# One cyclic table for the order of work on every engine, gated values split a stream at a time, and a convolution that runs further ahead

## The chip, the cores and the metric

The kernel runs on one NeuronCore of a Trainium2 chip. The core has five engines, each with a queue of its own that it works through strictly in order: TensorE (PE, matrix products into PSUM), VectorE (DVE), ScalarE (ACT), GpSimd (POOL) and SyncE (SP), which here issues nearly all the DMA transfers. Engines wait for one another through semaphores. The metric is the time of one execution on the device in microseconds (us). Three runs of the kernel before gave 443.19, 444.54 and 445.52, median 444.54. One more execution was profiled: it took 444.06, with a span of 442.2 from its first instruction to its last.

## The reference

An input `x` of 8 x 4224 tokens x 192 features goes through two convolutions over time, a gate and two products:

```python
w = softmax(weight)                      # 8 heads x 7 taps, one head per 24 features
out[b,s,h,:] = sum_k w[h,k] * x_pad[b,s+k,h,:]
x = out                                  # the first result is the input of the second part
gate_pre = sum_k conv_w[k] * xp[:, k:k+S, :]      # 5 taps, a weight per feature
gate = 1 / (1 + exp(-gate_pre))
val = x @ w_val                          # 192 x 192
result = (gate * val) @ w_out            # 192 x 192
```

## The kernel before, in words

**Tiling.** The 8 sequences are laid end to end, four to a row of blocks, so each block covers up to 488 tokens of two rows. There are 35 blocks (`STEPS`, numbered 0 to 34; the last has 380 tokens) in ten groups: group 0 has blocks 0 and 1, groups 1 to 8 four blocks each, group 9 the last. The 192 features times two rows make three *streams* of 128 partitions: streams 0 and 1 are the first 128 features of the two rows (together `x1`, one 976-wide tile), stream 2 holds the other 64 features of both rows (`x2`).

**First convolution.** It is made on PE, in units (`conv_unit`, L257): eight matmul records into one PSUM bank `pc` (L270), a copy by ACT into a buffer `e` (L276, six buffers), and one or two transfers that scatter `e` into `x1` or `x2` of the group (L280). Two of every three units belong to `x1`, the third to `x2`. A group of four blocks has 12 units, all units together are 106. After each third unit two more input tiles are loaded (`load_x`, L137; eight buffers, seven loaded at the start). `x1` and `x2` have three buffers, one for a group.

**Second convolution.** Each stream of each block has an accumulator in PSUM (`pg`, two banks for all). ACT makes the first tap into it (`tap0`, L315), DVE adds taps 1 to 4 (`tap`, L327), of which the last writes to `g` in SBUF; ACT then applies the sigmoid in place (L335; streams 0 and 1 in one instruction). So there are 12 taps on DVE for a block. Two taps of one stream are mostly set apart by a tap of the next (`taps`, L339).

**Products.** `val` and the output are products with a weight cut in four parts: `W11` and `W22` within the two feature ranges, `W12` and `W21` across. An f32 operand is split in two fp32r parts, a high one that ACT casts (`xh`, `ph`, L356) and a rest that POOL subtracts (`xl`, `pl`, L357), and each product is three matmuls. The 64-wide `W12` is used in plain f32 (`columns`, L393). The other parts are `rows` (`W21`, L402), `whole1` (`W11`, L411) and `whole2` (`W22`, L419). Every product of a block adds up in three banks, one for a stream: `pv` for the value, `po` for the output. `pv`, `po` and the convolution's `pc` share six banks, taken in turn: whoever opens a bank waits until the one opened six before has been read. DVE multiplies `pv` with the gate in place (`gated`, L432), ACT evacuates `po` into `ot` (L438), and SP stores a block's three streams with one transfer (L442).

**Order.** The order on every engine is written out by hand. `pair(n)` (L444) makes the value products of blocks n and n+1 and the output products of blocks n-1 and n, with six convolution units between its two halves. In its first half each product part of the value is followed by the same part of the output: `columns`, `rows`, `whole2`, `whole1`; in the second half the order is `whole1`, `whole2`, `rows`, `columns`. The gating of streams 0 and 1 of block n+1 follows `v2.rows` there. A prologue does 6, 3 and 3 units, then block 0's and block 1's first steps around six more, 18 units in all, so that units 12 to 17 come after block 0's taps and value product. Then come the pairs n = 1, 3, ..., 33 and an epilogue that makes the last block's output product. Group 1 (blocks 2 to 5, units 6 to 17) is first read early in pair 1, group 2 early in pair 5, and so on every second pair.

Of the kernel before, what the change touches and what calls it, by code (L numbers as in the profile page):

```python
# [7 lines left out]
F32 = mybir.dt.float32  # L8
F32R = mybir.dt.float32r
# [25 lines left out]
MB = 488  # L35
# [39 lines left out]
GROUP = [max(1, 4 // nj) for nj in NJS]  # L75
XW = 768
# [4 lines left out]
def kernel(  # L81
# [170 lines left out]
    def bank(name):  # L252
        return ps_v.tile([128, 512], F32, tag="pv", name=name)
# [3 lines left out]
    def conv_unit(g, u):  # L257
# [5 lines left out]
        pc = bank(f"pc_{g}_{u}")  # L263
        m, run = p.rows[i], p.wins[i] * WIN
        for k, h in enumerate(hs):
            t, o = xtiles[g, h]
            o += p.off[i]
            for w in range(p.wins[i]):
                c = k * run + w * WIN
                nc.tensor.matmul(  # L270
                    pc[:m, c : c + WIN], lhsT=t[:, o + w * m : o + w * m + m], rhs=band[:, h, :],
                    start=True, stop=True,
                )
        e = ep.tile([128, MB], F32, tag="e", name=f"e_{g}_{u}")
        n = run * len(hs)
        nc.scalar.copy(e[:m, :n], pc[:m, :n])  # L276
# [4 lines left out]

    units = [(g, u) for g in range(NG) for u in range(len(PLANS[g].units))]
    done = [0]

    def conv(k=1):
        for _ in range(k):
            if done[0] < len(units):
                g, u = units[done[0]]
                conv_unit(g, u)
                done[0] += 1  # L290
                i, hs = PLANS[g].units[u]
                if i == 1 and (hs[-1] + 1) % GROUP[g] == 0:
                    load_x(len(hs) // GROUP[g])
# [17 lines left out]
    def tap0(n, i):  # L311
        if n < N:
            m = STEPS[n][2]
            acc = accs[n, i] = ps_g.tile([128, 512], F32, tag="pg", name=f"pg_{n}_{i}")[:, :m]
            nc.scalar.mul(acc, unit_view(n, i, 0), cwt[:, i // 2, 0:1])  # L315

    def tap(n, i, k):
        if n >= N:
            return
# [12 lines left out]
    def sigmoid(n, i):  # L332
        if n < N:
            v = (g1s, g2s)[i][n]
            nc.scalar.activation(v, v, AF.Sigmoid)  # L335

    order = [(n, i) for n in range(1, N + 2) for i in (2, 0, 1)]

    def taps(n, i):  # L339


        k = order.index((n, i))
        nxt, opened = order[k + 1], order[k + 2]
        tap(n, i, 3)
        tap(*nxt, 1)
        tap(n, i, 4)
        tap(*nxt, 2)
        tap0(*opened)

    def split(pool, tag, n, i, x):  # L350
        m = STEPS[n][2]
        if i == 0:
            h, l = (pool.tile([128, 2, MB], F32R, tag=t, name=f"{tag}{t}_{n}")[:, :, :m] for t in ("h", "l"))
        else:
            h, l = (pool.tile([128, MB], F32R, tag=t, name=f"{tag}{t}_{n}")[:, :m] for t in ("h2", "l2"))
        nc.scalar.copy(h, x)  # L356
        nc.gpsimd.tensor_tensor(out=l, in0=x, in1=h.bitcast(F32), op=ALU.subtract)  # L357
        return h, l

    def split_x(n, i):  # L360
        if n < N:
            xs[n, i] = split(sp, "x", n, i, views(n)[i])

    def split_g(n, i):
        ps[n, i] = split(pp, "p", n, i, (g1s, g2s)[i][n])
# [3 lines left out]
    class Product:  # L369
# [18 lines left out]
        def columns(self):  # L388
# [9 lines left out]
        def rows(self):  # L398
# [8 lines left out]
        def whole1(self):  # L407
            first, both = self.open(0, 1)
            for q, acc in enumerate(both):
                for i, (a, b) in enumerate(self.passes(0)):  # L410
                    nc.tensor.matmul(  # L411
                        acc, lhsT=a[:, W11 : W11 + 128], rhs=b[:, q],
                        start=first and i == 0, stop=not first and i == 2,
                    )

        def whole2(self):
# [7 lines left out]
    def value(n):  # L424
        return Product(w_val, n, "pv", views(n)[0], xs, pvs)

    def output(n):
        return Product(w_out, n, "po", g1s[n], ps, pos)
# [5 lines left out]
    def evacuate(n, q):  # L434
        m = STEPS[n][2]
        if n not in ots:
            ots[n] = op.tile([128, 3 * MB], F32, tag="ot", name=f"ot_{n}")
        nc.scalar.copy(ots[n][:, q * m : (q + 1) * m], pos.pop((n, q)))  # L438

    def store(n, a=0, b=3):  # L440
        m = STEPS[n][2]
        nc.sync.dma_start(out[:, AT[n] + a * m : AT[n] + b * m], ots[n][:, a * m : b * m])  # L442

    def pair(n):  # L444
        m = n + 1
        v, o, v2, o2 = value(n), output(n - 1), value(m), None

        v.columns()
        split_g(n - 1, 1)
        taps(n, 0)  # L450
        o.columns()
        split_g(n - 1, 0)
        split_x(m, 0)
        v.rows()
        o.rows()
        taps(n, 1)
        sigmoid(n, 0)

        v.whole2()
        gated(n, 2)  # L460
        o.whole2()
        evacuate(n - 1, 2)
        split_x(m, 1)
        taps(m, 2)
        sigmoid(m, 1)
        v.whole1()
        split_g(n, 1)
        gated(n, 0)
        gated(n, 1)
        o.whole1()  # L470
        evacuate(n - 1, 0)
        evacuate(n - 1, 1)
        store(n - 1)
        split_g(n, 0)
        conv()
        taps(m, 0)
        conv(2)
        taps(m, 1)
        sigmoid(m, 0)
        conv(2)  # L480
        split_x(n + 2, 1)
        conv()
        split_x(n + 2, 0)
        taps(n + 2, 2)
        v2.whole1()
        o2 = output(n)
        o2.whole1()
        v2.whole2()
        o2.whole2()
        sigmoid(n + 2, 1)  # L490

        v2.rows()
        gated(m, 0)
        gated(m, 1)
        o2.rows()
        evacuate(n, 0)
        evacuate(n, 1)
        v2.columns()
        gated(m, 2)
        o2.columns()  # L500
        evacuate(n, 2)
        store(n)

    with tc.manual_schedule(engines={ENG.SP, ENG.PE, ENG.Activation, ENG.DVE, ENG.Pool}):
# [5 lines left out]
        conv(3)  # L510
        w_out.split()
        order[:0] = [(0, i) for i in (2, 0, 1)]
        tap0(0, 2)
        tap0(0, 0)
        split_x(0, 1)
        split_x(0, 0)
        tap(0, 2, 1)
        tap(0, 2, 2)
        taps(0, 2)
        conv(3)  # L520
        taps(0, 0)
        sigmoid(0, 1)
        v = value(0)
        v.columns()
        v.whole2()
        v.rows()
        v.whole1()
        for i in (1, 0):
            split_x(1, i)
        taps(0, 1)  # L530
        sigmoid(0, 0)
        conv(6)
        for q in (2, 0, 1):
            gated(0, q)
        taps(1, 2)
        sigmoid(1, 1)
        for n in range(1, N, 2):
            pair(n)
        split_g(LAST, 1)
        split_g(LAST, 0)  # L540
        o = output(LAST)
        o.columns()
        o.rows()
        o.whole2()
        evacuate(LAST, 2)
        store(LAST, 2, 3)
        o.whole1()
        for q in range(2):
            evacuate(LAST, q)
            store(LAST, q, q + 1)  # L550
# [68 lines left out]
```

## Time and profile before

| | |
|---|---|
| runs, median | 444.54 us (443.19 to 445.52) |
| profiled execution | 444.06 us, of it 442.2 span |
| mean granted TensorE clock | 0.956 |
| POOL, busiest line L357 | 122.3 us on `pl`, 112.0 us on `xl` |
| DVE, busiest line L327 | 218.6 us into `pg`, 75.0 us into `g` |
| HBM read, written | 28.33 MB, 26.01 MB |

The table of engines on the profile's page gives busy time, its share of the span and the number of instructions. PE is the matmuls, PEld the loading of their weights, which overlaps them. Names such as `po<-ph,woh` are what an instruction writes and reads. A bracket behind an instruction gives the idle time of its engine just before it, and what ended that. In the list of waits the three numbers are the total, how many times, and the longest.

### The profile page before, as it was taken

Reading aid. Unit: us, or ns where it says so; the run is one execution under the profiler, and the core shown is the slowest. Engines: PE = TensorE matmul, PEld = TensorE weight load, DVE = VectorE, ACT = ScalarE, POOL = GpSimd, SP = SyncE. Lnnn points to the kernel's source line nnn. Section 1 sums busy time; section 2 is a strip of 40 time slices with the busy share of each in tenths; the row PEclk is TensorE's granted clock in tenths of the full one; section 3 lists DMA queues with packets and bytes.
Section 4 is the critical chain, followed back from the end, with each engine's and each line's share of the span. In section 5 each row is a group of like instructions: output and inputs, shape, how many; then the busy total and the mean of one; then the engine's idle time right before and its main releaser. Section 6 shows DMA issues by size and latency. Waiting matters only on the chain.

```text
span 442.2 us, 7292 instructions
## 1 busy us (share of the span) xinstructions
PE 378.2 (86%) x2458; PEld 296.2 (67%) x2458; DVE 346.9 (78%) x572; ACT 322.2 (73%) x533; POOL 238.4 (54%) x155
## 2 busy tenths in 40 slices
PE   1758738999898989998898989898988898996965
PEld 1645527786777677867685959585957695864753
DVE  5159619797979597969797979797979797989851
ACT  2237419787888598859787988698869788887743
POOL 0215107564756384738473847384738473856652
PEclk9896967999999989999999999999999999998987
DMA  6899963939494939393949493939493936232113
GB/s 135 215 231 238 237 148 126 286 131 285 136 280 145 268 106 290 136 260 119 267 164 268 152 292 134 277 128 274 148 244 151 266 125 183 82 104 88 70 68 120
DMA packets 38805, 81.55 MB, mean 184 GB/s; under 512 B 7280, under 2 KB 25072, under 8 KB 38768
## 3 DMA queue, kind: packets, MB, share of 16 engines
q1 hardware_dynamic: 38512, 80.59, 64.3%
q0 software_dynamic: 256, 0.50, 0.5%
q8 instruction: 19, 0.31, 0.3%
q14 instruction: 18, 0.15, 0.1%
HBM read 28.33 MB, written 26.01 MB: 123 GB/s over the span
## 4 chain that ended last, share of the span: by engine, by line
PE 32%; DVE 20%; DMA 15%; issue 14%; ACT 11%; POOL 4%; SPq 2%; POOLq 0%; ACTq 0%; DVEq 0%
DMA x<-e 12%; DVE pg L327 11%; PE pc L270 6%; PE po L411 6%; DVE g L327 5%; DMA x<-xw 3%; PE pv L402 3%; PE pv L393 3%; ACT g L335 3%; POOL pl L357 3%; PE po L419 3%; PE pv L419 3%; DVE g L432 3%; ACT e L276 3%; PE po L402 3%
## 5 line engine op out<-in xcount | busy, mean ns | idle before, releaser
L327 DVE SCALAR_TENSOR_TENSOR pg<-x,cwt,pg 128x486 f32<-128x486 f32 (+2 forms) x315 | 218.6, 722 | 24.5 <-ACT pg L315 22.3
L357 POOL TENSOR_TENSOR pl<-g,ph 128x486 fp32r<-128x486 f32 (+2 forms) x70 | 122.3, 1747 | 106.8 <-ACT ph L356 100.1
L357 POOL TENSOR_TENSOR xl<-x,xh 128x486 fp32r<-128x486 f32 (+2 forms) x70 | 112.0, 1614 | 72.1 <-ACT xh L356 71.1
L270 PE MATMUL pc<-band,x 128*128 128x122 f32 (+1 forms) x848 | 104.3, 284 | 15.5 <-DMA band<-row 9.3
L270 PEld LDWEIGHTS pc<-band,x 128*128 128x128 f32 (+1 forms) x848 | 103.1, 200 | 18.1 <-issue 13.4
L315 ACT ACTIVATE pg<-x,cwt 128x488 f32<-128x488 f32 (+2 forms) x105 | 70.7, 673 | 60.3 <-DVE g L327 30.5
L432 DVE TENSOR_TENSOR g<-pv,g 128x488 f32<-128x488 f32 (+2 forms) x105 | 66.1, 658 | 44.6 <-PE pv L402 38.1
L438 ACT COPY ot<-po 128x488 f32<-128x488 f32 (+2 forms) x105 | 55.1, 558 | 30.0 <-PE po L402 14.0
L327 DVE SCALAR_TENSOR_TENSOR g<-x,cwt,pg 128x488 f32<-128x488 f32 (+2 forms) x105 | 75.0, 715 | 0.0
L276 ACT COPY e<-pc 128x488 f32<-128x488 f32 x106 | 56.8, 569 | 23.6 <-PE pc L270 14.6
L335 ACT ACTIVATE g<-g 128x486 f32<-128x486 f32 (+2 forms) x70 | 55.8, 798 | 1.7 <-DVE g L327 1.7
L356 ACT CAST xh<-x 128x486 fp32r<-128x486 f32 (+2 forms) x70 | 55.8, 803 | 0.0
L356 ACT CAST ph<-g 128x486 fp32r<-128x486 f32 (+2 forms) x70 | 55.4, 792 | 0.0
L411 PE MATMUL po<-ph,woh 128*128 128x486 f32 (+2 forms) x70 | 29.7, 424 | 26.4 <-ACT e L276 14.9
L393 PE MATMUL pv<-x,wvf 128*64 128x244 f32 (+2 forms) x280 | 36.4, 381 | 4.0 <-DMA x<-xw 4.0
L411 PE MATMUL po<-pl,woh 128*128 128x486 f32 (+2 forms) x70 | 29.8, 426 | 10.2 <-POOL pl L357 10.2
L411 PEld LDWEIGHTS po<-ph,woh 128*128 128x128 f32 x70 | 13.7, 196 | 34.9 <-ACT e L276 19.8
L393 PE MATMUL po<-g,wof 128*64 128x244 f32 (+2 forms) x280 | 34.4, 367 | 0.0
L393 PEld LDWEIGHTS pv<-x,wvf 128*64 128x64 f32 x280 | 18.7, 138 | 16.6 <-issue 10.0
L411 PE MATMUL pv<-xh,wvh 128*128 128x486 f32 (+2 forms) x70 | 29.0, 414 | 0.0
L411 PE MATMUL po<-ph,wol 128*128 128x486 f32 (+2 forms) x70 | 28.0, 399 | 0.0
L411 PE MATMUL pv<-xl,wvh 128*128 128x486 f32 (+2 forms) x70 | 27.5, 394 | 0.0
(67 smaller groups left out, 395.5 us busy)
## 6 DMA issues: line engine op xcount, KB each, us to landing
x<-xw SPq DMA_DIRECT2D x70, 384.0 KB, 6.1
x<-e SPq DMA_DIRECT2D x64, 244.0 KB, 5.3
out<-ot SPq DMA_DIRECT2D x18, 729.0 KB, 5.4
out<-ot SPq DMA_DIRECT2D x16, 732.0 KB, 3.2
x<-e SPq DMA_DIRECT2D x72, 122.0 KB, 5.8
out<-ot SPq DMA_DIRECT2D x3, 190.0 KB, 1.9
band<-row SPq DMA_DIRECT2D x8, 61.0 KB, 5.2
x<-e POOLq DMA_DIRECT2D x8, 61.0 KB, 7.6
```

Source lines behind the costliest of these rows:

```text
L270: nc.tensor.matmul(pc[:m, c : c + WIN], lhsT=t[:, o + w * m : o + w * m + m], rhs=band[:, h, :], start=True, stop=True,)
L276: nc.scalar.copy(e[:m, :n], pc[:m, :n])
L315: nc.scalar.mul(acc, unit_view(n, i, 0), cwt[:, i // 2, 0:1])
L327: nc.vector.scalar_tensor_tensor(out=dst, in0=unit_view(n, i, k), scalar=cwt[:, i // 2, k : k + 1], in1=acc, op0=ALU.mult, op1=ALU.add,)
L335: nc.scalar.activation(v, v, AF.Sigmoid)
L356: nc.scalar.copy(h, x)
L357: nc.gpsimd.tensor_tensor(out=l, in0=x, in1=h.bitcast(F32), op=ALU.subtract)
L393: nc.tensor.matmul(acc[p, c], lhsT=self.w.f[:, W12 : W12 + 64], rhs=self.x1[:, q, c], start=first and i == 0, stop=not first and i == 1,)
L402: nc.tensor.matmul(acc, lhsT=a[p, W21 : W21 + 128], rhs=b[p], start=first and i == 0, stop=not first and i == 2,)
L411: nc.tensor.matmul(acc, lhsT=a[:, W11 : W11 + 128], rhs=b[:, q], start=first and i == 0, stop=not first and i == 2,)
L432: nc.vector.tensor_tensor(out=v, in0=pvs.pop((n, q)), in1=v, op=ALU.mult)
L438: nc.scalar.copy(ots[n][:, q * m : (q + 1) * m], pos.pop((n, q)))
```

## The change

Four things change; what is computed stays the same.

1. *The table.* The hand-written `pair`, `taps` and most of the prologue and epilogue go. A text `SCHEDULE` lists the steps of a window, which again covers two blocks, n and n+1, and `window(n)` works through it for n = -5, -3, -1, 1, ..., 35, leaving out steps of blocks that don't exist. A step has a kind, an argument and an offset to n: `V` and `O` are value and output products with the part (`110` and `111` are `whole1` of stream 0 and of stream 1, now apart), `T` a tap (stream, tap), `Z` the first tap, `S` the sigmoid, `G` the gating, `E` the evacuation (a block's third one also stores), `CX` and `XL` cast and rest of `x` (1 or 2 for `x1` or `x2`), `CG` and `GL` cast and rest of the gated values, `U` the matmuls of a convolution unit, `K` its copy and scatter.
2. *Gated values a stream at a time.* `CG` and `GL` work on one stream, so that the 976-wide instructions of streams 0 and 1 become two of 488 each. The split of `x1` stays in one.
3. *Units in two parts.* `conv_unit` becomes `conv_begin` and `conv_end`, and in a window the copy of a unit comes one or two units after its matmuls.
4. *Further ahead.* 12 units come before window(-3) and six before window(-1); three more follow window(1) and three window(3). `U` and `K` do nothing in the windows up to -1. The table also casts `x1` one block earlier: `CX1+2` and `CX1+3` where the pair had n+1 and n+2.

By engine the table reads:

```
PE    V12+0 O12-1 V21+0 O21-1 V22+0 V110+0 V111+0 O22-1 O110-1 O111-1 U0 U1 U2 U3 U4 U5
      V110+1 V111+1 V22+1 O22+0 O110+0 O111+0 V21+1 O21+0 V12+1 O12+0
DVE   T11+0 T04+0 T12+0 T13+0 T21+1 T14+0 T22+1 G2+0 T23+1 G0+0 T24+1 T11+1 G1+0 T12+1 T01+1
      T13+1 T02+1 T14+1 T03+1 T04+1 T21+2 T22+2 T23+2 T01+2 T02+2 T24+2 T03+2 G0+1 G1+1 G2+1
ACT   CG2-1 E2-2 Z2+1 S2+0 CX2+1 CG1-1 S0+0 Z1+1 CX1+2 E2-1 CG0+0 Z0+1 K0 E0-1 K1 E1-1 K2 K3
      CG2+0 Z2+2 K4 CG1+0 K5 Z0+2 CX1+3 S2+1 S0+1 CX2+2 Z1+2 E0+0 CG0+1 E1+0
POOL  GL2-1 GL0-1 GL1-1 XL2+1 XL1+1 GL0+0 GL2+0 GL1+0 XL1+2 XL2+2
```

The core of the diff, with the lines that only rename left out:

```diff
+SCHEDULE = """
+    V12+0 T11+0 CG2-1 T04+0 E2-2 O12-1 GL2-1 T12+0 Z2+1 V21+0 T13+0 S2+0 GL0-1 O21-1 CX2+1 T21+1
+    CG1-1 T14+0 V22+0 GL1-1 T22+1 V110+0 S0+0 G2+0 V111+0 XL2+1 Z1+1 T23+1 O22-1 CX1+2 G0+0 O110-1
+    XL1+1 T24+1 E2-1 O111-1 T11+1 CG0+0 U0 Z0+1 G1+0 U1 T12+1 K0 GL0+0 E0-1 T01+1 U2 K1 T13+1 E1-1
+    U3 T02+1 K2 U4 T14+1 K3 T03+1 CG2+0 U5 Z2+2 GL2+0 T04+1 V110+1 K4 T21+2 CG1+0 V111+1 K5 T22+2
+    GL1+0 V22+1 Z0+2 T23+2 O22+0 CX1+3 XL1+2 T01+2 O110+0 S2+1 T02+2 O111+0 S0+1 T24+2 V21+1 CX2+2
+    T03+2 O21+0 Z1+2 XL2+2 G0+1 V12+1 G1+1 E0+0 CG0+1 O12+0 E1+0 G2+1
+"""
...
+    def part_g(n, q):
+        if q < 2:
+            return [t[:, q] for t in halves(ps, pp, "p", n, 0)] + [g1s[n][:, q]]
+        return halves(ps, pp, "p", n, 1) + [g2s[n]]
+
+    def cast_g(n, q):
+        h, _, x = part_g(n, q)
+        cast(h, x)
...
+    def window(n):
+
+        for step, arg, at in SCHEDULE:
+            if step == "U":
+                if n > 0:
+                    conv_begin()
+            elif step == "K":
+                if n > 0:
+                    conv_end()
+            elif 0 <= n + at < N:
...
-        conv(3)
+        conv(6)
         w_out.split()
...
+        window(-5)
+        window(-3)
         conv(6)
...
+        window(-1)
+        for n in range(1, N + 2, 2):
+            window(n)
+            if n < 4:
+                conv(3)
```

More of the change, by code (lines that the diff above doesn't have):

```diff
@@ L1 @@
+import re
 from contextlib import ExitStack
@@ L255, with conv_begin @@
     ISSUERS = {(0, 1): nc.gpsimd}
-    def conv_unit(g, u):
+    units = [(g, u) for g in range(NG) for u in range(len(PLANS[g].units))]
+    begun, ended, opened = [0], [0], {}
+    def conv_begin():
+        if begun[0] == len(units):
+            return
+        g, u = units[begun[0]]
+        begun[0] += 1
         p = PLANS[g]
@@ L273, in conv_unit, with conv_end @@
                 )
+    def conv_end():
+        if ended[0] == begun[0]:
+            return
+        g, u = units[ended[0]]
+        ended[0] += 1
+        p = PLANS[g]
+        i, hs = p.units[u]
+        m, run = p.rows[i], p.wins[i] * WIN
         e = ep.tile([128, MB], F32, tag="e", name=f"e_{g}_{u}")
         n = run * len(hs)
-        nc.scalar.copy(e[:m, :n], pc[:m, :n])
+        nc.scalar.copy(e[:m, :n], opened.pop((g, u))[:m, :n])
         dst = (x1s[g], x2s[g])[i].rearrange("p (s t) -> p s t", t=run)
@@ L405, in rows, with part11, part22 @@
                     )
[L407 to L416, printed above, removed]
+        def part11(self, q):
+            first, (acc,) = self.open(q)
+            for i, (a, b) in enumerate(self.passes(0)):
+                nc.tensor.matmul(
+                    acc, lhsT=a[:, W11 : W11 + 128], rhs=b[:, q],
+                    start=first and i == 0, stop=not first and i == 2,
+                )
+        def part22(self):
             first, (acc,) = self.open(2)
@@ L422, in whole2, with part, product @@
                 )
[L424 to L428, printed above, removed]
+        def part(self, k):
+            (self.part12, self.part21, self.part22)[("12", "21", "22").index(k)]() if len(k) == 2 else self.part11(
+                int(k[2])
+            )
+    products = {}
+    def product(kind, n, k):
+        if (kind, n) not in products:
+            products[kind, n] = (
+                Product(w_val, n, "pv", views(n)[0], xs, pvs) if kind == "V"
+                else Product(w_out, n, "po", g1s[n], ps, pos)
+            )
+        products[kind, n].part(k)
     def gated(n, q):
@@ L436, in evacuate @@
         if n not in ots:
[L437 to L502, printed above, removed]
@@ new lines, in evacuate @@
+            ots[n] = op.tile([128, 3 * MB], F32, tag="ot", name=f"ot_{n}"), []
+        ot, full = ots[n]
+        nc.scalar.copy(ot[:, q * m : (q + 1) * m], pos.pop((n, q)))
+        full.append(q)
+        a, b = (q, q + 1) if n == LAST else (0, 3) if len(full) == 3 else (0, 0)
+        if b:
+            nc.sync.dma_start(out[:, AT[n] + a * m : AT[n] + b * m], ot[:, a * m : b * m])
+    STEP = {"V": product, "O": product, "G": gated, "E": evacuate, "Z": tap0, "T": tap, "S": sigmoid,
+            "CX": cast_x, "XL": rest_x, "CG": cast_g, "GL": rest_g}
```

117 lines of the change are left out of this document (37 added, 80 removed).

## Prediction, with its working

> **What bounds the kernel now.** I read the page first, then the busy time by stage (the windows view), then who waited for whom, then one pair of blocks in order of time, and last the two ends of the span.
>
> ```profile
> span 442.2 us, 7292 instructions
> PE 378.2 (86%) x2458; PEld 296.2 (67%) x2458; DVE 346.9 (78%) x572; ACT 322.2 (73%) x533; POOL 238.4 (54%) x155
> ```
>
> No engine fills the span, so the stages have to be looked at one by one. I cut the span where `v.columns` of pair 3 and of pair 33 begin. Columns: length, then busy time of PE, PEld, DVE, ACT, POOL, then the granted clock, DMA share and GB/s.
>
> ```profile
> 0.00:83.73 83.73, 52.98 (x307) 43.48 (x309) 46.51 (x99) 39.86 (x67) 25.42 (x27) 0.86 0.84 195
> 83.73:413.59 329.86, 304.68 (x2038) 238.15 (x2036) 286.74 (x452) 268.36 (x442) 200.44 (x120) 0.99 0.64 189
> 413.59:442.20 28.61, 20.55 (x117) 14.57 (x113) 13.68 (x25) 14.02 (x24) 12.53 (x8) 0.86 0.25 99
> ```
>
> The middle row is pairs 3 to 31, fifteen of them: 329.86 / 15 = 21.99 us a pair. PE is busy 304.68 / 15 = 20.3 of it, DVE 19.1, ACT 17.9. So three engines stand close together and PE is nearest to full. What keeps them from being full is seen in the waits:
>
> ```profile
> DVE g L432 <- PE pv L402: 38.1, 17, 5.4
> DVE pg L327 <- ACT pg L315: 22.3, 7, 10.7
> ACT pg L315 <- DMA x<-e: 16.3, 3, 11.8
> PE po L411 <- ACT e L276: 14.9, 12, 1.3
> ```
>
> Once a pair, DVE waits for `v2.rows` before it can gate (38.1 / 17 = 2.2 us), and in most pairs PE waits over a microsecond for a bank that ACT's convolution copy gives back. One pair in order of time:
>
> ```profile
> 300.47 0.49 PE L411 MATMUL po<-ph,woh 128*128 128x486 f32 x1 [1.12 <-ACT e L276]
> ...
> 305.98 0.99 PE L393 MATMUL pv<-x,wvf 128*64 128x242 f32 x8
> ...
> 310.68 0.38 PE L411 MATMUL pv<-xh,wvh 128*128 128x486 f32 x1
> ...
> 313.35 5.51 PE L270 MATMUL pc<-band,x 128*128 128x122 f32 x48
> ...
> 318.63 0.47 PE L411 MATMUL pv<-xh,wvh 128*128 128x488 f32 x1
> ...
> 322.18 0.49 PE L411 MATMUL po<-ph,woh 128*128 128x486 f32 x1 [1.30 <-ACT e L276]
> ```
>
> The same matmul returns after 322.18 - 300.47 = 21.71, and it waited 1.30, so without that wait PE needs 20.41 for a pair. Its parts: one half's products 313.35 - 305.98 = 7.37, the six convolution units 318.63 - 313.35 = 5.28, or 0.88 a unit. DVE over the same pair:
>
> ```profile
> 300.90 0.72 DVE L327 SCALAR_TENSOR_TENSOR pg<-x,cwt,pg 128x486 f32<-128x486 f32 x1
> 303.77 1.24 DVE L432 TENSOR_TENSOR g<-pv,g 128x488 f32<-128x488 f32 x2 [2.15 <-PE pv L402]
> 305.37 0.67 DVE L432 TENSOR_TENSOR g<-pv,g 128x488 f32<-128x488 f32 x1 [0.36 <-PE pv L393]
> ...
> 315.38 1.36 DVE L327 SCALAR_TENSOR_TENSOR pg<-x,cwt,pg 128x488 f32<-128x488 f32 x2
> 316.64 0.72 DVE L327 SCALAR_TENSOR_TENSOR g<-x,cwt,pg 128x488 f32<-128x488 f32 x1
> 317.28 2.13 DVE L327 SCALAR_TENSOR_TENSOR pg<-x,cwt,pg 128x488 f32<-128x488 f32 x3
> 319.31 0.72 DVE L327 SCALAR_TENSOR_TENSOR g<-x,cwt,pg 128x488 f32<-128x488 f32 x1
> ...
> 322.60 0.72 DVE L327 SCALAR_TENSOR_TENSOR pg<-x,cwt,pg 128x486 f32<-128x486 f32 x1
> ```
>
> From 300.90 to 322.60 it is 21.70, of which 2.15 + 0.36 are waits: 19.19 of work. One tap starts 0.63 after the other (316.64 - 315.38 for two), but where a tap follows the one before it on the same accumulator it costs 0.77 (319.31 - 317.28 = 2.03 for three, one of them so).
>
> Pairs longer than 21.7 are those where the chain runs through a scatter of convolved data into `x1`:
>
> ```profile
> 191.40 7.52 DMA x<-e
> ...
> 279.82 6.90 DMA x<-e
> ```
>
> These land just when the next group of four blocks is first read, so about every second pair is longer. The head has the same wait at its largest:
>
> ```profile
> 64.31 0.67 ACT L315 ACTIVATE pg<-x,cwt 128x488 f32<-128x488 f32 x1 [11.82 <-DMA x<-e]
> 65.02 0.73 DVE L327 SCALAR_TENSOR_TENSOR pg<-x,cwt,pg 128x488 f32<-128x488 f32 x1 [10.75 <-ACT pg L315]
> 65.96 0.77 PE L411 MATMUL po<-ph,woh 128*128 128x486 f32 x1 [7.24 <-ACT ph L356]
> ```
>
> **The change part by part.**
>
> *The table in the steady pairs.* PE's work is the same instructions, so its 20.41 stays. I follow one window from `V12+0` at 0, PE without gaps: products of the first half to 7.4, `U0` to `U5` 0.88 apart to 12.7, second half to 20.2. The wait on `v2.rows` goes because `V21+1` (ends near 17.6) now has seven taps of block n+2 on DVE ahead of `G0+1`; what is late next is `G2+1`, which needs `V12+1` (ends near 19.2): 0.4 us left of the former 2.5. DVE's own time is 19.19 and two more dependent neighbours (five such pairs in the table where the old order has three), 2 x 0.14: 19.5, with the 0.4 it is 19.9, below PE's 20.4. The wait of PE for ACT's copies goes because `K0` to `K3` now each follow two units behind their `U`: `K3` is through near 11.7 and `O22+0` wants its bank at 14.7. `K4` and `K5` near 13.1 and 14.1 for 15.4 and 16.1.
>
> The tightest meetings I find are on the two `pg` banks. A `Z` can start only after the last tap of the accumulator two before it, and `Z2+2` stands on ACT behind `K3` and `CG2+0`: it ends at about 12.7, DVE wants it at 12.4, so 0.3 us late. The other five end 0.3 or more early. Bounds of these six: nothing, or up to half a microsecond each, 3.0 a window; I take 0.3 because in the old order DVE's wait for ACT's first tap (22.3 us, 7 times, above) holds 10.75 in a single wait of the head, and pairs like the one shown have none.
>
> *Gated values a stream at a time.* The 972-wide cast and subtraction of each block become two of 486:
>
> ```profile
> L356 ACT CAST ph<-g 128x972 fp32r<-128x972 f32 x18 | 18.2, 1009 | 0.0
> L356 ACT CAST ph<-g 128x486 fp32r<-128x486 f32 x18 | 10.5, 582 | 0.0
> L357 POOL TENSOR_TENSOR pl<-g,ph 128x972 fp32r<-128x972 f32 x18 | 40.8, 2266 | 19.6 <-ACT ph L356 19.0 <-PE pc L270 0.7
> L357 POOL TENSOR_TENSOR pl<-g,ph 128x486 fp32r<-128x486 f32 x18 | 22.1, 1230 | 14.1 <-ACT ph L356 8.1 <-POOL xl L357 6.1
> ```
>
> That is 2 x 0.582 - 1.009 = 0.16 us more on ACT and 2 x 1.230 - 2.266 = 0.19 more on POOL a block, 0.3 and 0.4 a pair. ACT then does 17.9 + 0.3 = 18.2, POOL 200.44 / 15 + 0.4 = 13.8, both under 20.4, so the cost is nothing while PE bounds; without that cover it would be 0.3 x 17 = 5 us. In return `O110` waits for 1.2 us of POOL instead of 2.3. The scatters, loads and stores keep their number; SP issues a unit's scatter after its `K`, and one store falls between `K1` and `K2`, whose scatters wait on SP for it by a few tenths and are not read for over a window.
>
> *Convolution ahead.* In the steady pairs a group is complete a window before it is first read, so the long pairs go. The price: units 12 to 17 stand ahead of block 0's taps on ACT, and three units run between windows 1 and 3 and three between 3 and 5. Such a run is 3 x 0.88 = 2.6 us of PE, and then `V12` of the next window needs the bank that `E2` frees, which there stands on ACT behind the run's last copy and `CG2`:
>
> ```profile
> L438 ACT COPY ot<-po 128x488 f32<-128x488 f32 (+2 forms) x105 | 55.1, 558 | 30.0 <-PE po L402 14.0
> L276 ACT COPY e<-pc 128x488 f32<-128x488 f32 x106 | 56.8, 569 | 23.6 <-PE pc L270 14.6
> ```
>
> 0.569 + 0.582 + 0.558 = 1.7 more. So 2.6 at best, 4.3 at worst; I take 4.3 each. They come back at the end, where windows 29, 31 and 33 have no unit left instead of 31 and 33.
>
> *The head.* When group 1 has landed is set by transfers that the change does not alter:
>
> ```profile
> 56.00:60.00 4.00, 2.73 (x7) 1.78 (x6) 0.00 (x0) 0.00 (x0) 0.00 (x0) 0.69 1.03 209
> ...
> 64.00:68.00 4.00, 1.18 (x2) 0.50 (x2) 2.98 (x5) 3.69 (x5) 2.01 (x1) 0.50 0.03 10
> 68.00:72.00 4.00, 3.71 (x14) 3.42 (x15) 4.00 (x8) 3.76 (x8) 4.00 (x4) 0.50 0.01 4
> ```
>
> The DMA engines are full (share 1.03) and the order on SP is the same. In window(-1) the only reader of group 1 is `CX1+3`, the cast of block 2's `x1`. It can start a little before 64.31, say 63.4, since it does not need the last unit. Behind it on ACT stand `S2` and `S0` of block 0, and on DVE all three gatings of block 0 wait for those: 63.4 + 0.9 + 0.6 + 1.0 = 65.9, three gatings to 67.7. So block 0's output product, of which three quarters are done at 65 now, has not begun, and neither have block 1's value products but the first. PE starts near 67 with the clock at 0.50, as it does now from 65.96; until 72 it did half its work, and I count some 2.5 us for that. This puts the zero of window 1 at about 69, some 5 us behind the old order at the same work.
>
> The rows give 0.50 for 64 to 72, some 6 us after PE starts again. [...]
>
> *The end.*
>
> ```profile
> 388.70:410.00 21.30, 17.42 (x94) 12.42 (x95) 20.10 (x32) 16.94 (x27) 14.36 (x9) 0.92 0.26 93
> ```
> ```profile
> 425.19 0.61 DVE L327 SCALAR_TENSOR_TENSOR g<-x,cwt,pg 128x380 f32<-128x380 f32 x1
> 431.17 1.01 DVE L432 TENSOR_TENSOR g<-pv,g 128x380 f32<-128x380 f32 x2 [5.36 <-PE pv L402]
> ```
>
> A pair without convolution takes 21.3 now; in the table nothing but DVE's 19.5 is left to bound it. In the last pair DVE waits 5.36 for `v2.rows`; in window 33 `V21` of block 34 comes some 1.8 after the last tap, and with `CG2`, `GL2` first another 1.5 goes: 28.61 - 3.6 - 1.5 = 23.5.
>
> *The sum*: 69 + 2 x (20.4 + 4.3) + 11 windows (5 to 25) x 20.4 + 3 (27, 29, 31; 27 has four units left) x 19.5 + 23.5 = 69 + 49.4 + 224.4 + 58.5 + 23.5 = 424.8 of span. The profiled run took 444.06 for 442.2, so 426.7 beside it; the median is 444.54, 0.5 above, so 427.
>
> **The rivals.**
>
> *Half of it stays.* If three more of the six first taps come 0.3 late, DVE takes 19.9 + 0.3 + 0.9 = 21.1 a window: 14 x 0.7 = 10 more, 437. For it: ACT passes 32 instructions a window in strict order, waiting in between. Against: the margins above.
>
> *Slower.* The two `pg` banks decide: with copies, casts and evacuations placed between ACT's first taps, each of the six comes 0.4 late, and DVE takes 19.9 + 2.4 = 22.3. Then a window is as long as a pair is now, or longer, and the 5 us of the head and the 8.6 of the extra runs stay unpaid: 427 + 14 x 1.9 = 454. It turns to slower from a window of about 21.8. Against it: five of the six are early by my walk.
>
> *No change*: windows of 21.5 to 21.8, 442 to 446, if the table only trades one wait for another, as a pair without the long scatter wait takes 21.7 now.
>
> *DVE bounds instead of PE.* If PE's matmuls could stand closer than its busy time shows, windows would take DVE's 19.5: 427 - 13 x 0.9 = 415. Against it: the products of half a pair take 7.37 from start to start with no wait between them, as the rows at 305.98 and 313.35 show. [...]
>
> **How the numbers follow.** A window bound by PE, 427 (its own range 421 to 433): 0.66. Half: 0.15. Slower: 0.09. No change: 0.05. DVE: 0.05. The first two make 0.81; from the best head and runs (421, and 3 less for the runs' lower bound) to the upper edge of the half case: 418 to 440. A change of 0.5% (2.2 us) is about what a measurement can tell from none: faster 0.66 + 0.15 + 0.05 = 0.86, same 0.05, slower 0.09.
>
> **What would show it.** Right: windows 20.2 to 20.6 apart; no wait of `g` for `pv L402` over half a microsecond; no wait of `po` for `e`; PE busy over 97% between windows 5 and 25; no DMA `x<-e` in the chain after the head; a gap of 4 us in DVE after windows 1 and 3; block 0 gated near 66. Wrong: a repeated wait of `pg` on DVE for ACT, a window over 21.3, or first gatings after 70.

## The result and the profile after

| | before | after |
|---|---|---|
| median of 4 runs each, same chip | 443.87 us (440.82 to 445.52) | 412.86 us (412.01 to 416.94) |
| ratio, 95% interval | | 0.9327 (0.9246 to 0.9408) |
| profiled execution, of it span | 444.06, 442.2 us | 413.00, 411.2 us |

The change takes 31 us, or 6.7%. The forecast was 427 with a range from 418 to 440, so the sign was right and the gain was much too small. (Some executions are over 1.5% slower than the fastest of their kernel, and medians, ranges and ratios leave these out; two traces further down are of such executions, the old kernel with its copies first and the table with one run, and no verdict rests on the totals of these two.)

The head of the page of the kernel after, with the busy time of the engines:

```profile
span 411.2 us, 7389 instructions
...
PE 370.8 (90%) x2458; PEld 296.5 (72%) x2458; DVE 350.2 (85%) x572; ACT 326.3 (79%) x568; POOL 243.6 (59%) x190
```

The matmuls and DVE's instructions are as many as before. ACT and POOL have 35 more each, one for each block whose gated pair is split in two, and 4.1 and 5.2 us more work. Of the 31.0 us of span, 23.6 are time in which PE stood still (442.2 - 378.2 = 64.0 before, 411.2 - 370.8 = 40.4 after); in the other 7.4 PE is busy for less time with as many matmuls, in a full window 20.01 us where a pair of the old kernel had 20.3.

I cut the kernel after where the forecast cut its sum: the zero of a window is the start of `V12+0`. Busy time by stage (length, PE, PEld, DVE, ACT, POOL, granted clock, DMA share, GB/s):

```profile
0.00:64.43 64.43, 34.15 (x177) 29.19 (x177) 27.41 (x68) 22.82 (x39) 11.02 (x19) 0.81 0.93 207
64.43:110.31 45.88, 45.71 (x320) 37.54 (x319) 41.10 (x65) 39.19 (x69) 27.87 (x21) 1.00 0.80 195
110.31:330.41 220.10, 220.10 (x1542) 180.00 (x1542) 211.43 (x329) 201.92 (x353) 151.28 (x110) 1.00 0.86 232
330.41:388.50 58.09, 52.59 (x310) 36.66 (x308) 57.19 (x91) 48.61 (x82) 40.48 (x30) 0.97 0.24 91
388.50:411.20 22.70, 18.22 (x117) 13.07 (x113) 13.12 (x24) 13.72 (x27) 12.97 (x11) 0.99 0.31 125
```

The third row is windows 5 to 25, eleven of them: 220.10 / 11 = 20.01 us each, and PE is busy 220.10 of 220.10. The clock is 1.00 throughout. DVE stands at 211.43 / 220.10 = 96%, ACT at 92%. In the row behind it, windows 27, 29 and 31, in which the convolution runs out, DVE takes over: 57.19 of 58.09.

(The first cut, 64.43, is where window 1 would have begun with a full clock: the zero of window 3 at 87.30, less one run of 2.87 and one window of 20.0. All heads below are reckoned so.)

Waits of the kernel after (total, times, longest):

```profile
DVE pg L351 <- ACT pg L341: 13.6, 6, 8.9
...
DVE g L469 <- PE pv L422: 4.2, 12, 0.4
...
ACT xh L373 <- DMA x<-e: 4.2, 2, 2.1
...
PE po L422 <- DVE g L469: 3.4, 1, 3.4
```

The wait of `g` for `v2.rows`, 38.1 us before, has no row any more; it left 0.4 a window on `V12+1`, as forecast. PE no longer waits for ACT's copies before an output product. Of DVE's waits for a first tap, 8.9 of 13.6 are one wait of the head.

One window in order of time, on PE and then on DVE:

```profile
210.37 0.99 PE L422 MATMUL pv<-x,wvf 128*64 128x242 f32 x8
...
217.74 5.51 PE L294 MATMUL pc<-band,x 128*128 128x122 f32 x48
223.02 0.47 PE L439 MATMUL pv<-xh,wvh 128*128 128x488 f32 x1
...
230.38 0.99 PE L422 MATMUL pv<-x,wvf 128*64 128x242 f32 x8
```

```profile
228.76 0.66 DVE L469 TENSOR_TENSOR g<-pv,g 128x488 f32<-128x488 f32 x1
229.78 0.67 DVE L469 TENSOR_TENSOR g<-pv,g 128x488 f32<-128x488 f32 x1 [0.36 <-PE pv L422]
...
238.52 2.62 DVE L351 SCALAR_TENSOR_TENSOR pg<-x,cwt,pg 128x488 f32<-128x488 f32 x4
```

From zero to zero it is 230.38 - 210.37 = 20.01, made of 7.37 + 5.28 + 7.36, and no PE row carries a bracket. These are the very parts that the old trace showed for one half (7.37) and six units (5.28).

### The profile page after: what moved, and what is told of

Same layout as the page of the kernel before. It is cut to its first block, busy times and chain, and to the rows that moved or that the text cites. A ratio compares the mean times of both kernels' runs of the same rounds, so it can differ in the third digit from the quotient of the medians.

```text
span 411.2 us, 7389 instructions
## 1 busy us (share of the span) xinstructions
PE 370.8 (90%) x2458; PEld 296.5 (72%) x2458; DVE 350.2 (85%) x572; ACT 326.3 (79%) x568; POOL 243.6 (59%) x190
## 4 chain that ended last, share of the span: by engine, by line
PE 74%; DMA 10%; DVE 7%; SPq 2%; issue 2%; ACT 2%; POOL 1%; DVEq 0%; POOLq 0%
PE pc L294 21%; PE po L439 10%; PE pv L439 9%; PE pv L431 6%; PE pv L422 6%; PE po L422 6%; PE pv L447 5%; PE po L431 5%; PE po L447 5%; DMA x<-xw 5%; DVE pg L351 4%; DMA x<-e 4%; SPq L197 2%; DVE g L469 2%; POOL pl L376 1%
## 5 line engine op out<-in xcount | busy, mean ns | idle before, releaser
L351 DVE SCALAR_TENSOR_TENSOR pg<-x,cwt,pg 128x486 f32<-128x486 f32 (+2 forms) x315 | 219.6, 723 | 16.2 <-ACT pg L341 13.6
L376 POOL TENSOR_TENSOR pl<-g,ph 128x488 fp32r<-128x488 f32 (+2 forms) x105 | 128.2, 1230 | 99.1 <-ACT ph L373 98.9
L376 POOL TENSOR_TENSOR xl<-x,xh 128x972 fp32r<-128x972 f32 (+3 forms) x70 | 112.4, 1618 | 44.5 <-ACT xh L373 44.5
L294 PE MATMUL pc<-band,x 128*128 128x122 f32 (+1 forms) x848 | 108.2, 289 | 19.6 <-DMA band<-row 9.0
L309 ACT COPY e<-pc 128x488 f32<-128x488 f32 x106 | 60.4, 575 | 44.2 <-PE pc L294 25.8
L373 ACT CAST ph<-g 128x488 fp32r<-128x488 f32 (+2 forms) x105 | 62.6, 597 | 2.6 <-DVE g L469 2.2
L476 ACT COPY ot<-po 128x488 f32<-128x488 f32 (+2 forms) x105 | 59.0, 565 | 6.0 <-PE po L431 3.6
L373 ACT CAST xh<-x 128x972 fp32r<-128x972 f32 (+1 forms) x70 | 55.3, 791 | 4.7 <-DMA x<-e 4.2
L422 PEld LDWEIGHTS po<-g,wof 128*64 128x64 f32 x280 | 20.1, 136 | 12.7 <-DVE g L469 4.2
L439 PE MATMUL po<-ph,woh 128*128 128x486 f32 (+2 forms) x70 | 26.8, 383 | 1.3 <-ACT ph L373 1.3
L439 PE MATMUL pv<-xh,wvl 128*128 128x486 f32 (+2 forms) x70 | 26.8, 383 | 0.0
```

What stands on the lines that cost most here:

```text
L294: nc.tensor.matmul(pc[:m, c : c + WIN], lhsT=t[:, o + w * m : o + w * m + m], rhs=band[:, h, :], start=True, stop=True,)
L309: nc.scalar.copy(e[:m, :n], opened.pop((g, u))[:m, :n])
L351: nc.vector.scalar_tensor_tensor(out=dst, in0=unit_view(n, i, k), scalar=cwt[:, i // 2, k : k + 1], in1=acc, op0=ALU.mult, op1=ALU.add,)
L422: nc.tensor.matmul(acc[p, c], lhsT=self.w.f[:, W12 : W12 + 64], rhs=self.x1[:, q, c], start=first and i == 0, stop=not first and i == 1,)
L439: nc.tensor.matmul(acc, lhsT=a[:, W11 : W11 + 128], rhs=b[:, q], start=first and i == 0, stop=not first and i == 2,)
L476: nc.scalar.copy(ot[:, q * m : (q + 1) * m], pos.pop((n, q)))
```

## The experiments

There are twelve runs (the kernel after and the one with its extra units in the head stand among them a second time); in the diffs `...` stands for lines left out. Each ratio is to the kernel before on the same chip. To keep the head, which differs from run to run, out of a comparison of tables, I also use the stretch from the zero of window 3 to the end: 411.2 - 87.30 = 323.9 us in the kernel after.

### Parts of the change in the old order

Copies first: the six copies of a pair stand ahead of the first half's sigmoid, in the old kernel.

```diff
-        conv(2)
+        conv(4)
         taps(m, 1)
         sigmoid(m, 0)
-        conv(2)
```

> The old order with one move: the fourth and fifth convolution units of a pair stand ahead of the taps of stream 1 (and so their copies ahead of the first tap and the sigmoid that ACT makes there). Theory A: the old pair was a closed loop over three engines (DVE's tap, ACT's first tap and sigmoid, ACT's copy, PE's bank for the output product, v2.rows, DVE's gating); with the copy ahead PE no longer waits 1.3 us for its bank, pairs without a late scatter go from 21.7 to 20.2 to 20.6, and the time from 444 to 420 to 428. Theory B: DVE's wait for v2.rows has its own cause, in the place of the gatings behind the products, and only the whole table removes it: pairs stay above 21.3 and the time above 437.

Measured: 439.1 us, ratio 0.9888 (0.9831 to 0.9944), a gain of about 1%. Two pairs of its profile, one after the other:

```profile
135.76:156.55 20.79, 20.30 (x142) 16.28 (x140) 19.09 (x32) 18.09 (x30) 12.90 (x8) 1.00 0.71 204
156.55:180.97 24.42, 22.13 (x142) 17.64 (x140) 19.18 (x32) 18.07 (x30) 13.91 (x8) 0.93 0.73 204
```

A good pair falls from 21.7 to 20.8, nearly as far as theory A has it (20.2 to 20.6), but every second one stays longer (the clock of the one shown was 0.93, so its length is no measure of the wait alone). So little of the gain comes out, and the time is in theory B's range.

Lead alone: three units more after pairs 1 and 3 of the old kernel.

```diff
             pair(n)
+            if n < 4:
+                conv(3)
```

> The old order with three more convolution units after pair 1 and three after pair 3, so that a group is complete earlier. Theory A (the order of the table is the gain, the lead only takes the late scatters away): the long pairs become 21.7, which is about 4 us less over fifteen pairs, two runs cost 2.9 each, so 441 to 447. Theory B (the lead is the gain): long waits for scatters go and 430 or less.

Measured: 440.2 us, ratio 0.9897 (0.9856 to 0.9937), just under A's 441. Its pairs are alike:

```profile
131.32:153.04 21.72, 20.43 (x143) 16.20 (x140) 19.09 (x32) 18.18 (x30) 12.91 (x8) 1.00 0.78 219
153.04:174.77 21.73, 20.44 (x142) 16.23 (x140) 19.09 (x32) 18.19 (x30) 14.02 (x8) 1.00 0.72 208
```

So the long pairs of the old kernel came from too little lead, and the 21.7 of a good pair is its order. (By the starts of `v.columns`, four of the old kernel's fifteen pairs are long, 22.6 to 23.9 us, and not every second one, as the forecast read it.)

Both together:

> The old order with two edits together: the six copies of a pair stand ahead of the first half's sigmoid, and three units more run after pairs 1 and 3. Theory A (a pair is a loop through PE, ACT and DVE, and the early copies take PE's 1.3 us out of it; the long pairs come from the missing lead): every pair now as long as the good ones of the early-copies run, 20.8 us, so 15 x (21.99 - 20.8) = 18 us less, two runs of 2.9 more, about 430 us, ratio 0.965 to 0.975. Theory B (the two gains are one and the same): about 440, ratio 0.985 to 0.99. Neither expects 413: DVE's wait of 2.2 us a pair for v2.rows stays in this order.

Measured: 431.24 us, ratio 0.9648 (0.9586 to 0.9709). The two gains of 1% make 3.5% when both are there, for each alone leaves the wait that the other removes. Pairs are 20.8 throughout, ten of them in the first row here, and the last four with the end in the second:

```profile
128.61:336.54 207.93, 203.03 (x1402) 162.95 (x1400) 190.84 (x302) 180.83 (x300) 134.46 (x80) 1.00 0.77 217
336.54:426.80 90.26, 74.69 (x425) 53.47 (x421) 70.82 (x115) 62.05 (x100) 52.16 (x32) 0.90 0.23 90
```

And with the gated values of streams 0 and 1 split one at a time as well:

```diff
     def split_g(n, i):
-        ps[n, i] = split(pp, "p", n, i, (g1s, g2s)[i][n])
+        ...
+        for q in range(2):
+            nc.scalar.copy(h[:, q], x[:, q])
+            nc.gpsimd.tensor_tensor(out=l[:, q], in0=x[:, q], in1=h[:, q].bitcast(F32), op=ALU.subtract)
+        ...
```

> The old order with all that can be had without the table: copies ahead of the sigmoid, three units more after pairs 1 and 3, and the gated values of the first two streams split one at a time. Theory A (pairs of 20.8 us in this order are a loop of PE, ACT and DVE in which O110 does not wait for POOL; the split helps only where the table has put O110 close behind the gating): pairs stay at 20.7 to 20.9, 429 to 433 us, and the table itself is worth the 18 us that are left. Theory B (the split is worth its 26 us in any order): pairs of 20.0 to 20.2, 415 to 421 us.

Measured: 424.83 us, ratio 0.9547 (0.9486 to 0.9608). Its same two stretches:

```profile
131.50:340.24 208.74, 202.95 (x1402) 162.95 (x1400) 190.82 (x302) 182.56 (x320) 137.10 (x100) 1.00 0.76 217
340.24:424.70 84.46, 71.90 (x425) 51.10 (x421) 70.53 (x115) 62.61 (x109) 53.45 (x41) 0.96 0.25 96
```

The pairs stay at 20.87, as theory A has it, but the total fell below its 429: with the split the last pairs, which have no convolution to cover POOL, take 90.26 - 84.46 = 5.8 us less. I had not looked there. PE's waits for POOL's rests in that stretch fall from 5.4 to 3.0 us; its clock rose from 0.90 to 0.96 as well, and what is left of the 5.8 is not told apart. What holds the steady pairs at 20.9 is in this kernel's waits from 131.5 to 340.24:

```profile
DVE g L441 <- PE pv L411: 13.3, 10, 1.3
...
PE po L428 <- ACT e L276: 5.8, 10, 0.6
```

Both are in every pair: the wait for `v2.rows`, and half a microsecond for ACT's copies. These two are what is left for the table.

### Parts of the change taken out of the table

The gated values of streams 0 and 1 split together, behind the second gating (`CG0` and `GL0` do nothing, `CG1` and `GL1` take both streams):

```diff
         if q < 2:
-            return [t[:, q] for t in halves(ps, pp, "p", n, 0)] + [g1s[n][:, q]]
+            return halves(ps, pp, "p", n, 0) + [g1s[n]]
...
     def cast_g(n, q):
-        h, _, x = part_g(n, q)
-        cast(h, x)
+        if q:
+            h, _, x = part_g(n, q)
+            cast(h, x)
...
     def rest_g(n, q):
-        rest(*part_g(n, q))
+        if q:
+            rest(*part_g(n, q))
```

> The table with the casts and rests of gated streams 0 and 1 joined again into one 976-wide instruction each, at the place of stream 1. Theory A (splitting lets the output product of stream 0 start with 1.2 us of POOL behind it): O110 of the second half waits some 0.6 us for its third pass in each window with convolution, 8 us more than the 413 of the changed kernel, 417 to 425. Theory B (the split has no part in it): within 2 us of 413.

Measured: 438.2 us, ratio 0.9899 (0.9862 to 0.9935). Theory A has the right place but 13 us too little at its upper end, 425; B falls. The profiled run took 433.82 (432.0 of span); each of its steady windows takes 21.0. Where, on PE:

```profile
211.01 0.39 PE L441 MATMUL po<-ph,wol 128*128 128x486 f32 x1
212.04 0.48 PE L441 MATMUL po<-pl,woh 128*128 128x486 f32 x1 [0.65 <-POOL pl L376]
```

The third pass of `O110`, the one that reads the rest, waits for POOL's long subtraction. From one pass to the next it is 212.04 - 211.01 = 1.03 in place of 0.22, which is 0.81 of the 1.0 that a window grew, and as PE had no slack each window is longer: 255.9 us against 243.1 from the zero of window 3 to that of window 27, and 89.6 against 80.8 from there to the end; the head was 0.8 shorter, 20.8 in all. The median lies 4.4 us above the profiled run, and there is no trace that shows where, so that part stays open.

No units ahead between windows 1 and 5:

```diff
             window(n)
-            if n < 4:
-                conv(3)
```

> The table without the two runs of three units between windows, so that the convolution is six units less ahead. Theory A (the table needs the lead, because it casts x1 of block n+3 at 14.7 us of a window, while the group's last unit is only copied at 14 and lands 8 us later): every second window waits 5 to 7 us, seven of them, less 5.7 for the runs, so 435 to 455. Theory B (there is slack enough behind that cast): 5 to 7 us less than 413, 406 to 410.

Measured: 471.82 us, ratio 1.0631 (1.0556 to 1.0707): slower than the kernel before. Its waits:

```profile
ACT xh L373 <- DMA x<-e: 65.7, 8, 10.8
DVE g L469 <- ACT g L358: 61.3, 9, 10.3
...
PE pv L422 <- DVE g L469: 46.6, 8, 8.6
```

The mechanism is A's, its price larger than the 455 that A had at most. Eight times, once a group, `CX1+3` waits for a scatter at the head of ACT's queue, 65.7 / 8 = 8.2 us; the sigmoids stand behind it, the gatings wait for these, and PE for the banks (46.6 / 8 = 5.8). The table casts `x1` a block earlier than the pair did, so it needs the lead.

### How much lead, and where

One run only, after window 1 (`if n < 2`):

> The changed kernel with the run of three units after window 1 alone; the one after window 3 is dropped, so that convolution is 15 units less far ahead by half of what the two runs give. Theory A (one run's lead is enough but for about 2 us of slack, as in window 3 of the changed kernel where CX1 waited 2.1 us for a scatter and PE lost 0.14): 2.9 us of run saved, three units later at the end in a window that is then bound by PE at 20.0 instead of 19.0, so 410 to 413 us. Theory B (every second window again waits on its scatters, as without any run, where each lost 8 to 10 us, here less by the 10 us that half a window's lead gives): 8 windows of 1 to 4 us more, 420 to 440 us.

Measured: 407.89, 414.48, 415.87 and 416.67 us, with the kernel before at 445.9. They are too far apart to tell A's 410 to 413 from the kernel after, and three have no trace. The profiled one (415.87, span 414.1) has the zero of window 3 at 93.00 instead of 87.30, and from there to the end it takes 321.1, 2.8 less than the kernel after, with no long windows. In that stretch it is theory A: the second run buys nothing. Without a run between windows at all, three units in the head instead:

```diff
+                if n == -1 and step == "CX" and b == 2:
+                    for _ in range(3):
+                        conv_end()
 ...
+        for _ in range(3):
+            conv_begin()
         window(-1)
 ...
-            if n < 4:
-                conv(3)
```

> The changed kernel without either run between windows; instead three units' matmuls are begun ahead of the first steps of block 0, where PE stands idle from 46 to 54 us, and their copies stand on ACT just ahead of the cast of block 2, where ACT is idle for 2 us. Theory A (the run's price is PE's time, which is free here, and one run's lead is nearly enough): the zero of window 1 some 0 to 2 us later, two runs of 2.9 us saved, windows at 20.0 to 20.3: 408 to 413 us. Theory B (one run's lead is not enough): every second window 1 to 4 us longer, 8 of them, 418 to 440 us. Theory C (the head's transfers are the bound, and three more units' scatters put off group 1): the zero of window 1 3 us later or more, the rest as in A: 412 to 417.

Measured: 408.0 us (407.49 to 411.16), ratio 0.9154 (0.9085 to 0.9223). The stretch from window 3 to window 27 of this kernel:

```profile
84.53:324.60 240.07, 240.07 (x1683) 196.28 (x1681) 232.43 (x362) 219.94 (x384) 164.59 (x120) 1.00 0.84 229
```

Twelve windows of 20.01 with PE full from the first on; the lead of one run is enough, and in the head it costs nothing, since PE stands idle there: window 1 begins at 84.53 - 20.0 = 64.5, where the kernel after has 64.4. The same kernel beside the unedited kernel after, on one chip:

> The version without runs between the windows, whose three extra units stand in the head, once more, beside the changed kernel on one chip. Theory A (the two runs cost 2 x 2.9 us and their lead is worth no more than that of one run): 4 to 6 us below the changed kernel of the same call, 407 to 410 us. Theory B (its first lead over the changed kernel was an early landing in the head): within 2 us of it.

> The changed kernel once more, unedited, beside the next ones on one chip. Theory A (its head is set by when the transfers of group 1 land, and that differs from run to run: the sixteenth scattered unit landed at 60.6 us in its first profile, at 64.8 in the profile with one run, whose head is the same program): single times spread over 410 to 418 us, and the begin of the window after window 1 lies 25 to 29 us behind that landing in any profile. Theory B (the head is the same each time): all within 1 us of 412.9.

Measured: 411.6 us (408.57 to 413.14) against 415.13 (412.26 to 416.06), ratios 0.9249 (0.9192 to 0.9305) and 0.9327 (0.9276 to 0.9379). The medians are 3.5 us apart, a little under A's 4 to 6, and 411.6 lies just above A's 407 to 410; the profiled spans are 406.8 and 413.1. The times of the kernel after spread as its theory A has it, over 3.8 us. This version is the fastest here of those that leave nothing out.

### What bounds a window

One of three passes left out of `part11`, 1.77 us of PE's work a window (the output lacks that term):

```diff
             for i, (a, b) in enumerate(self.passes(0)):
+                if i == 1:
+                    continue
```

> The changed kernel with one of the three passes of the quarter product part11 left out, for values and outputs: eight matmuls of about 0.22 us a window, 1.77 us less work for PE, so that what it computes lacks that term. Theory A (PE's 20.0 us bound a window and nothing else does): windows fall until DVE's 19.2 to 19.5 bind, that is by 0.5 to 0.8 us each, some 14 of them, and the head and end by under 1 each: 400 to 406 us, ratio to the kernel before 0.90 to 0.915, PE's busy share in windows 5 to 25 falls to 93 to 96%, and DVE's rises above 98%. Theory B (windows stand at 20.0 because of a loop over PE, ACT and DVE whose waits don't show, or the full DMA engines): windows stay at 20.0, 411 to 413 us, and PE shows gaps of 1.7 us a window.

Measured: 406.79 us, ratio 0.9117 (0.9058 to 0.9176). Ten of its windows:

```profile
150.12:342.77 192.65, 188.68 (x1306) 145.68 (x1305) 190.88 (x301) 182.87 (x319) 137.13 (x100) 1.00 0.82 223
```

They take 19.27 instead of 20.01: less work on PE shortens the window at once, until DVE is full (190.88 of 192.65). PE bounds the window, and the next bound is 0.74 us below it. One window near the head, in which DVE is not yet full, shows the whole of it:

```profile
112.77:131.06 18.29, 18.29 (x133) 14.94 (x134) 16.62 (x27) 17.85 (x32) 14.25 (x10) 1.00 1.05 287
```

With PE full, 1.72 of the 1.77 us come off. The total, 406.79, lies just above A's upper figure because of the head, whose window 3 begins at 90.18 here and at 87.30 in the kernel after; from there to the end it is 314.3 us against 323.9. PE's busy share is still 98%, where A had 93 to 96: a busy share near full is no proof of a bound by itself, the shorter window is.

### The head

Units 12 to 17 put back to about where the old order has them:

```diff
+                if n == -1 and step == "CX" and b == 2:
+                    conv(6)
 ...
         window(-3)
-        conv(6)
         window(-1)
```

> The changed kernel with units 12 to 17 put back in the head to about where the old order has them: ahead of the cast of block 2, behind the first taps and casts of blocks 0 and 1, instead of ahead of everything of block 0. Theory A (group 1 lands when the queue of transfers, eight deep on SP, comes to it, whenever the copies are made): within 2 us of the changed kernel of the same call, the sixteenth unit landing between 60 and 65 us. Theory B (the head was 4.6 us shorter than forecast because those copies stand earlier): 2 to 5 us slower.

Measured: 418.07 us (415.62 to 419.67), ratio 0.9399 (0.9344 to 0.9453), against 415.13 for the kernel after beside it: 2.9 us slower, theory B. The chain of waits of the kernel after in its first profile, in its second, and of this one shows the last scatter and what follows it (start, length):

```profile
53.98 6.92 DMA x<-e
60.90 0.99 ACT xh L373
```

```profile
51.02 9.85 DMA x<-e
62.13 1.42 ACT g L358 x2
64.30 2.45 PE po L422 x8
```

```profile
52.68 5.88 PE pc L294 x48
59.60 6.79 DMA x<-e
67.62 1.42 ACT g L358 x2
69.79 2.45 PE po L422 x8
```

The scatter ends at 60.9, 60.9 and 66.4. In the last chain it is issued only at 59.60, behind the convolution's matmuls on PE: the place of units 12 to 17 (their matmuls as well as their copies) does move the landing. In the first profile it was the transfers: SP issues at 44.72 and again at 53.98, each time just after the transfer that it issued eight before has landed (the one of 35.30 at 44.65, the one of 44.72 at 53.97). In the two profiles of the same kernel it lands alike, and yet the zero of window 3 comes at 87.30 in one and 89.63 in the other. From the end of that scatter to the zero it is 26.4 and 28.8, and 27.8 in the kernel with the late units, inside the 25 to 29 that theory A of the kernel after had for any head; but its cause, a landing that differs from run to run, does not tell these two profiles apart. The difference between the two is seen in PE's first product after the wait, in the first profile and in the second:

```profile
64.06 1.61 PE L422 MATMUL po<-g,wof 128*64 128x242 f32 x8 [3.40 <-DVE g L469]
```

```profile
64.30 2.45 PE L422 MATMUL po<-g,wof 128*64 128x242 f32 x8 [5.91 <-DVE g L469]
```

The first had idled 3.40 us and ran at clock 1.00, the second 5.91 and ran at 0.50. It starts 0.24 us later (64.30 for 64.06), so of the 2.33 us between the two zeros 2.09 come behind it.

## Why the prediction was wrong

Its mechanism held: PE bounds the windows, the long pairs are gone, the extra runs and the later head cost a little. Its cases are told apart by the windows, and the likeliest one came true in kind. Two of its signs missed: windows 20.2 to 20.6 apart (20.01) and the first gatings near 66 (63.33). The 13.6 us of span between 424.8 and 411.2 are sizes of its terms:

| term | forecast | measured | difference |
|---|---|---|---|
| head, to the zero of window 1 | 69 | 64.4 | -4.6 |
| windows 1 and 3 with their runs | 49.4 | 45.9 | -3.5 |
| eleven windows, 5 to 25 | 224.4 | 220.1 | -4.3 |
| windows 27, 29, 31 | 58.5 | 58.1 | -0.4 |
| end | 23.5 | 22.7 | -0.8 |

**The window, 20.41 for 20.01.** The step that failed: "it waited 1.30, so without that wait PE needs 20.41 for a pair". The bracket is not what the wait cost. On PE of the kernel before:

```profile
320.49 0.39 PE L411 MATMUL po<-pl,woh 128*128 128x486 f32 x1
322.18 0.49 PE L411 MATMUL po<-ph,woh 128*128 128x486 f32 x1 [1.30 <-ACT e L276]
322.50 0.38 PE L411 MATMUL po<-ph,wol 128*128 128x486 f32 x1
```

The 1.30 count from the end of the row before, 320.49 + 0.39, but a pass that does not wait starts 0.22 after the one before it (320.49 - 320.27), ahead of that end. From start to start it is 322.18 - 320.49 = 1.69, so the wait cost 1.47, and the pass behind it takes 0.32 to the next start, another 0.10. One first pass of `O22` is 0.11 longer in the same way (from 301.90 to 302.23). So 21.71 - 1.47 - 0.10 - 0.11 = 20.03. The rows beside it had the answer too: 2 x 7.37 + 5.28 = 20.02. The kernel that leaves out 1.77 us shows that this sum is a real floor, since PE's work and nothing else had to shrink. It is worth 0.4 x 13 = 5 us in all, and the forecast's own two ways to the number should have been set against each other.

**The runs, 4.3 for 2.87.** The forecast took the worse end: "`V12` of the next window needs the bank that `E2` frees". On PE and ACT of the kernel after:

```profile
84.43 2.94 PE L294 MATMUL pc<-band,x 128*128 128x122 f32 x24
87.30 1.04 PE L422 MATMUL pv<-x,wvf 128*64 128x242 f32 x8
```

```profile
88.37 0.57 ACT L476 COPY ot<-po 128x486 f32<-128x486 f32 x1
```

`V12` begins at 87.30, a microsecond before that evacuation starts, and with no bracket; it did not need that bank, though by a count of six banks in turn it should have, and why is open. What waits for ACT's evacuation is the weight load of `V21` at 89.09, by 0.36 us. With two runs that is 2.9 us, and 0.6 more comes from the window itself.

**The head, 69 for 64.4.** The step that failed: "When group 1 has landed is set by transfers that the change does not alter". The earlier units do alter when SP may issue; put back, they cost 2.9 us. The cast of block 2 started at 60.90 where the forecast had 63.4. The other 2 us are, by an estimate from the two profiles of the kernel after, the clock: the forecast counted 2.5 us for a start at 0.50, and the second profile, which has one, loses 2.09 us behind its first product. So the price was about right, and it was luck of the first profile that it did not have to pay it. With one run only, the same head landed at 64.8 in its profile and put the zero of window 1 at 70.1. The forecast's 69 lies among what this head does, not at its middle.

Which clock PE had behind its wait does not go by the length of the wait alone in these traces. In the two profiles of the kernel after it was 1.00 behind 3.40 us and 0.50 behind 5.91; in the first profile of the kernel with its extra units in the head PE had waited only 1.88 us, and the clock was 0.62 in the microsecond from 58 and 0.50 from 60 to 68.

```profile
57.93 1.63 PE L422 MATMUL pv<-x,wvf 128*64 128x242 f32 x8 [1.88 <-ACT e L309]
```

```profile
58.00:59.00 1.00, 1.00 (x8) 0.55 (x8) 0.96 (x3) 1.00 (x3) 0.00 (x0) 0.62 1.07 239
```

Nor did the half clock last equally long behind the first product. In the second profile of the kernel after it lasted from 64.30 to between 70 and 71, some 6 us, as in the old kernel (65.96 to 72.1); in the second profile of the one with its extra units in the head, where the clock had already been 0.64 from 60 to 64, it was over after 3.2 us (64.72 to 67.9). The second profile of the kernel after, in that microsecond:

```profile
70.00:71.00 1.00, 1.00 (x5) 0.88 (x4) 0.02 (x1) 0.91 (x2) 1.00 (x2) 0.69 0.00 0
```

**The extra neighbours, the `pg` banks, the split's cost on ACT and POOL** came to nothing on the path, as forecast. In steady windows no first tap shows among DVE's large waits, so the slower rival had nothing to stand on. The DVE gaps behind the runs are 2.5 and 1.4 us instead of 4.

**The rival of 415** was nearest in time and wrong in cause: DVE at 96% does not bound, as the kernel with less work for PE shows. Nor is the bound to be read from PE's weight loads here: PEld stands at 180.00 / 220.10 = 82% in the stretch where PE is busy for 220.10 of 220.10.

**What the range lacked.** The three errors lie on one side and add up. The lower edge, 418, was made of the best head and the cheap runs; it had no room for a window of 20.0.

**Where the 31 us come from**, going from the old order to the new, with the ratios applied to 446: copies earlier and lead together 446 to 430 (0.9648), the split 430 to 426 (0.9547), the table 426 to 416 (0.9327). In the profiles of the last two on one chip, with spans of 424.7 and 413.1, ten windows give 208.74 - 200.05 = 8.7 us and the stretch behind them 84.46 - 80.34 = 4.1, and the head up to them takes 1.2 back (131.50 and 132.71). Taken the other way, out of the table, the split is worth some 25 us and the lead 58 (0.9899 and 1.0631 less 0.9327, of 446). Shares depend on the order, because each part removes a wait that hides another.

## What to carry to other kernels

Where one engine is to become the bound, work out its floor from the starts of groups that run back to back, without a bracket, and price a wait by the distance between starts, not by its bracket (here 1.47 us where the bracket had 1.30). Price each part of a change together with what it uncovers: two edits worth 1% each gave 3.5% together, and the table without its lead was slower than the old kernel. Work that an order needs ahead of time belongs where its engine is idle anyway (three units in the head in place of six between the windows saved 3.5 us).

## What the hardware showed that was not expected

- PE was kept busy without a gap: 220.10 of 220.10 us over 1542 matmul records at clock 1.00, in windows of 20.01 that are the sum of their back-to-back parts, with the DMA engines at a share of 0.86 beside it.
- With PE full, a lateness of under a microsecond became time in every window: the 0.65 us wait in `O110` made windows of 21.0 out of 20.0.
- The same program's head differed by several microseconds from run to run (zero of window 3 at 87.30 and 89.63 in the kernel after, at 93.00 in the profile with one run), and with it the clock: with the last scatter at 60.9 in both profiles of the kernel after, the clock behind PE's wait was 1.00 in one and 0.50 in the other, and window 3 began 2.3 us apart.
- How long PE had waited did not tell by itself what clock it got: a fall to 0.50 behind 1.88 us in the kernel with its extra units in the head, 1.00 behind 3.40 us in the kernel after. Nor did one figure give the way back: 3.2 us of half clock behind the first product in one profile, some 6 us in two others.
